# Holding back the first weight load, and moving tile 3's transposes into the fifth weight tile, in a fused LayerNorm + S5 + Mish MLP kernel

## The chip, the cores and the metric

One core of one Trainium2 chip. The metric is the device time of one execution in microseconds (us). Before the change it was 621.98 us, the median of three runs (621.54 to 622.13).

## The reference

```python
x  = A_x                                   # (1, 2048, 1024) bf16
xn = layernorm(x)                          # per token, over 1024
# A: diagonal complex state-space layer, 1024 states, plus a skip
Lam_bar = exp(dt * Lam);  B_bar = ((Lam_bar - 1) / Lam)[:, None] * Bmat
h_t = Lam_bar * h_{t-1} + B_bar @ xn_t
A   = 2 * Re(C h) + xn * Dskip
# B: dense, Mish, dense; w1 is 1024 x 3584, w2 is 3584 x 1024
z   = xn @ w1 + b1
B   = (z * tanh(softplus(z))) @ w2
out = x + A + B
```

## The kernel before

Tokens are worked in four blocks of 512, each block as four x tiles of 128 tokens. In each block TensorE does `xn @ w1` (28 weight tiles of 8 matmuls), the state-space input projection (128 matmuls), and then the second dense layer together with the output projection (352 matmuls). Weights come from HBM through a ring of seven slots; the first four weight tiles need slots 0 (contraction rows 0 to 511) and 1 (rows 512 to 1023), the next four slots 2 and 3.

TensorE does the matrix products and the transposes, VectorE and ScalarE the statistics, the scaling and the copies, and SyncE issues the loads. Only block 0's start-up matters here. Loads are issued in this order:

```python
    for h in range(2):                       # x tile 0, in two halves of the columns
        SP.dma(... xx[:, 0, 0, h * 512:(h + 1) * 512] ...)
    load_x(SP, 0, 1)                         # x tile 1
    ...
    for i in range(NRING):
        ring_load()                          # weight load i, 512 KB
        if i == 0:
            load_x(SP, 0, 2)                 # x tiles 2 and 3 behind weight load 0
            load_x(SP, 0, 3)
        ...
```

TensorE begins with filler matmuls on an identity matrix, so that they and not the real work take the slow stretch at the start: in the profile before, a 128-column filler took 107 ns up to 5.93 us and 56 ns from there. VectorE takes the statistics of tiles 0 and 1, scales them, and TensorE transposes them. Tiles 2 and 3 arrive later, so the first weight tiles are cut in two token halves: the first 256 tokens need only x tiles 0 and 1.

```python
    keep_busy(48)                            # filler: 128-column matmuls
    PE.op(... transpose of the small parameters ...)
    keep_busy(12)
    ...                                      # statistics, scale, transposes, copies of tiles 0 and 1
    first_mean_a(3)                          # ScalarE: sum of tile 3
    ...
    NSPLIT = 5
    def first_half(f, half, k0=0, k1=NK):    # 256 tokens of weight tile f: one matmul per k
        ...
    for f in range(4):
        first_half(f, 0, 0, NK // 2)         # 16 matmuls, weight load 0
    for f in range(4):
        first_half(f, 0, NK // 2, NK)        # 16 matmuls, weight load 1
        if f in (1, 3):
            q = 2 + f // 2
            first_transpose(q)               # tiles 2 and 3
            first_copy(q, VE)
    for f in range(4, NSPLIT):
        first_half(f, 0)
    ...                                      # then first_half(f, 1) for f < NSPLIT, whole tiles after
```

## Time and profile before

| | before |
|---|---|
| time, median of 3 | 621.98 us |
| profiled execution: time, span | 622.33 us, 620.9 us |
| share of TensorE in the chain of waits | 98% |
| x tile 1 landed (trace) | 5.50 us |
| first weight matmul | 9.46 us |

The first view is the chain of waits of the kernel before: start, length, what ended last there. Read it downwards. Everything up to 9.46 us is one dependence: x tile 1's load, its statistics, its scaling, the copy of its transpose. From there the chain is TensorE's own work nearly to the end, with one gap of 0.04 us at 13.66.

```profile
...
1.72 3.79 DMA xx<-in_A_x_dram
...
5.53 0.70 DVE stats L348
...
7.91 0.73 DVE xn L376 x2
8.64 0.67 DVE xnT L401 x2
...
9.46 2.78 PE ps L516 x24
...
14.32 5.33 PE ps L516 x48
19.64 39.71 PE ps L661 x184
59.36 27.63 PE ps L682 x128
...
```

The second view is the timeline of TensorE's matmuls (start, time, line, shapes, count). L388 are transposes, L516 the half-token matmuls, L661 the whole weight tiles.

```profile
...
9.46 2.78 PE L516 MATMUL ps<-xnT,ring 128*128 128x256 bf16 x24
12.17 0.62 PE L388 MATMUL ps<-ident,xn 128*128 128x128 bf16 x8
12.62 1.04 PE L516 MATMUL ps<-xnT,ring 128*128 128x256 bf16 x8
13.70 0.62 PE L388 MATMUL ps<-ident,xn 128*128 128x128 bf16 x8
14.16 5.49 PE L516 MATMUL ps<-xnT,ring 128*128 128x256 bf16 x48
19.48 2.75 PE L661 MATMUL ps<-xnT,ring 128*128 128x512 bf16 x12
```

The third is the timeline of the weight loads into TensorE's array (PEld), which adds in brackets how long that unit sat idle and what ended it.

```profile
...
12.16 0.45 PEld L388 LDWEIGHTS ps<-ident,xn 128*128 128x128 bf16 x8 [0.21 <-DVE xn L376]
...
13.69 0.45 PEld L388 LDWEIGHTS ps<-ident,xn 128*128 128x128 bf16 x8 [0.32 <-DVE xn L376]
...
15.10 4.26 PEld L516 LDWEIGHTS ps<-xnT,ring 128*128 128x128 bf16 x40 [0.19 <-DVE xnT L401]
...
```

### The profile page before, as it was taken

Reading aid. Unit: us, or ns where it says so; the run is one execution under the profiler, and the core shown is the slowest. Engines: PE = TensorE matmul, PEld = TensorE weight load, DVE = VectorE, ACT = ScalarE, POOL = GpSimd, SP = SyncE. Lnnn points to the kernel's source line nnn. Section 1 sums busy time; section 2 is a strip of 40 time slices with the busy share of each in tenths; the row PEclk is TensorE's granted clock in tenths of the full one; section 3 lists DMA queues with packets and bytes.
Section 4 is the critical chain, followed back from the end, with each engine's and each line's share of the span. In section 5 each row is a group of like instructions: output and inputs, shape, how many; then the busy total and the mean of one; then the engine's idle time right before and its main releaser. Section 6 shows DMA issues by size and latency. Waiting matters only on the chain.

```text
span 620.9 us, 7382 instructions
## 1 busy us (share of the span) xinstructions
PE 616.8 (99%) x2961; PEld 287.4 (46%) x2961; DVE 462.3 (74%) x676; ACT 247.9 (40%) x161; POOL 50.7 (8%) x47
## 2 busy tenths in 40 slices
PE   8999999999999999999999999999999999999998
PEld 7544444444444444444444444444444444444444
DVE  6897899999457599998147759999624856999603
ACT  5689996440069940000008992000000999000000
POOL 1999000000100000000010000000000000000000
DMA  9999966850365400784054430276203552033001
GB/s 293 258 269 258 220 110 187 207 150 0 117 193 165 136 0 25 209 191 119 17 187 135 141 131 1 75 209 170 90 35 103 163 176 68 1 123 115 1 0 69
DMA packets 95805, 79.41 MB, mean 128 GB/s; under 512 B 48923, under 2 KB 78235, under 8 KB 95771
## 3 DMA queue, kind: packets, MB, share of 16 engines
q1 hardware_dynamic: 92272, 71.64, 42.4%
q10 hardware_dynamic: 2538, 4.14, 1.8%
q0 software_dynamic: 960, 3.15, 1.6%
q8 instruction: 24, 0.39, 0.3%
q14 instruction: 11, 0.08, 0.0%
HBM read 63.19 MB, written 4.19 MB: 109 GB/s over the span
## 4 chain that ended last, share of the span: by engine, by line
PE 98%; DVE 1%; DMA 1%; SPq 0%; issue 0%
PE ps L740 49%; PE ps L661 30%; PE ps L682 18%; PE ps L516 1%; DMA xx<-in_A_x_dram 1%; DVE stats L348 0%; PE ps L754 0%; DVE xn L376 0%; PE ps L388 0%; SPq L291 0%; DVE xnT L401 0%; DVE xx L808 0%; DVE mv L353 0%; DVE par L495 0%; DVE rs L372 0%
## 5 line engine op out<-in xcount | busy, mean ns | idle before, releaser
L740 PE MATMUL ps<-ring,act 128*128 128x512 bf16 x896 | 194.0, 379 | 0.0
L661 PE MATMUL ps<-xnT,ring 128*128 128x512 bf16 x856 | 185.4, 379 | 0.0
L640 ACT ACTIVATE act<-hb 128x3584 bf16<-128x3584 bf16 x16 | 51.0, 3185 | 224.2 <-DVE hb L669 223.8
L740 PEld LDWEIGHTS ps<-ring,act 128*128 128x128 bf16 x896 | 87.7, 98 | 105.7
L661 PEld LDWEIGHTS ps<-xnT,ring 128*128 128x128 bf16 x856 | 83.7, 98 | 100.8
L669 DVE TENSOR_SCALAR hb<-ps,par 128x512 bf16<-128x512 f32 x112 | 82.5, 747 | 55.9 <-PE ps L661 54.7
L682 PE MATMUL ps<-xnT,BT 128*128 128x512 bf16 x512 | 111.2, 379 | 0.0
L740 PE MATMUL ps<-CT,hT 128*128 128x512 bf16 x506 | 109.9, 379 | 0.0
L687 DVE TENSOR_TENSOR mt<-ps,tab 128x1024 bf16<-128x1024 f32 x64 | 75.4, 1220 | 17.2 <-PE ps L682 16.6
L682 PEld LDWEIGHTS ps<-xnT,BT 128*128 128x128 bf16 x512 | 50.1, 98 | 60.4
L740 PEld LDWEIGHTS ps<-CT,hT 128*128 128x128 bf16 x506 | 49.5, 98 | 59.7
L705 DVE TENSOR_TENSOR_SCAN hT<-cs,qi,hT 128x512 bf16<-128x512 f32 x48 | 58.9, 1269 | 0.0
L785 DVE TENSOR_TENSOR xx<-ps,xx 128x1024 bf16<-128x1024 f32 (+1 forms) x16 | 18.8, 1190 | 46.3 <-PE ps L740 46.2
L642 ACT ACTIVATE act<-act 128x3584 bf16<-128x3584 bf16 x16 | 51.1, 3192 | 0.2
L641 ACT ACTIVATE act<-act 128x3584 bf16<-128x3584 bf16 x16 | 51.1, 3192 | 0.2
L710 DVE TENSOR_TENSOR mt<-hT,tab 128x1024 bf16<-128x1024 bf16 x64 | 41.4, 688 | 1.1
L647 DVE TENSOR_TENSOR act<-act,hb 128x3584 bf16<-128x3584 bf16 x16 | 32.3, 2018 | 1.3 <-ACT act L642 1.3
L287 POOL DMA_DIRECT2D xx<-in_A_x_dram x12 | 6.7, 560 | 253.2 <-DVE xx L785 146.2
L616 ACT ACTIVATE ct<-CT,cs 128x512 f32<-128x512 bf16 x16 | 11.5, 721 | 26.6 <-DVE CT L618 25.9
L641 ACT ACT_TABLE_LOAD x16 | 20.5, 1283 | 0.3
L642 ACT ACT_TABLE_LOAD x16 | 20.5, 1283 | 0.3
L705 DVE TENSOR_TENSOR_SCAN hT<-cs,hT 128x512 bf16<-128x512 f32 x16 | 18.7, 1209 | 0.0
(85 smaller groups left out, 276.8 us busy)
## 6 DMA issues: line engine op xcount, KB each, us to landing
ring<-in_B_w_dram SPq DMA_DIRECT2D x112, 512.0 KB, 4.1
out_dram<-xx ACTq DMA_DIRECT2D x15, 256.0 KB, 2.1
xx<-in_A_x_dram POOLq DMA_DIRECT2D x12, 256.0 KB, 3.6
xx<-in_A_x_dram SPq DMA_DIRECT2D x3, 256.0 KB, 4.9
xx<-in_A_x_dram SPq DMA_DIRECT2D x2, 128.0 KB, 2.2
dsk<-in_A_Dskip_dram SPq DMA_DIRECT2D x1, 256.0 KB, 8.4
xnT<-xn SPq DMA_TRANSPOSE x12, 4.7
BT<-in_A_B_re_dram SPq DMA_TRANSPOSE x8, 5.9
```

The costliest lines, as they stand in the source:

```text
L640: aop(lambda e: e.activation(a, hs, AF.Exp), reads=[b_hb[g % 2]], writes=[b_act[g]])
L641: aop(lambda e: e.activation(a, a, AF.Ln, bias=1.0), reads=[b_act[g]], writes=[b_act[g]])
L642: aop(lambda e: e.activation(a, a, AF.Tanh), reads=[b_act[g]], writes=[b_act[g]])
L647: vop(lambda e: e.tensor_tensor(a, a, hs, op=ALU.mult), reads=[b_act[g], b_hb[g % 2]], writes=[b_act[g]])
L661: PE.mm(lambda e, k=k, w=w: e.matmul(ps[:, bank, :], lhsT=w, rhs=xnT[:, k, :], start=k == 0, stop=k == NK - 1), reads=[b_ring[s]] + b_xnT, ...
L669: vop(lambda e: e.tensor_scalar(hb[:, hs, :], ps[:, bank, :], b1(f), None, op0=ALU.add), reads=[b_ps[bank], b_par], writes=[b_hbf[hs]])
L682: PE.mm(lambda e, j=j, ci=ci, k=k, bank=bank: e.matmul(ps[:, bank + ci, :], lhsT=BT[:, ci, j, k, :], rhs=xnT[:, k, :], start=k == 0, stop= ...
L687: vop(lambda e, s=s, u=u, j=j: e.tensor_tensor(mt[:, s, :, :], u, tab[:, s, j, :].unsqueeze(1).to_broadcast([P, 2, TB]), op=ALU.mult), rea ...
L705: vop(lambda e, ci=ci, init=init: e.tensor_tensor_scan(out=hT[:, ci, j, :], data0=cj("r", j).to_broadcast([P, TB]), data1=hT[:, ci, j, :], ...
L710: vop(lambda e, s=s: e.tensor_tensor(mt[:, s, :, :], hT[:, :, j, :], tab[:, s, j, :].unsqueeze(1).to_broadcast([P, 2, TB]), op=ALU.mult), ...
L740: PE.mm(lambda e: e.matmul(ps[:, u, :], lhsT=lhsT, rhs=rhs, start=st_, stop=last), reads=reads, writes=[b_ps[u]], first=st_, last=last)
L785: vop(lambda e: e.tensor_tensor(xr, src, xr, op=ALU.add), reads=b_ps[bank:bank + n] + [b_x], writes=[b_x])
```

## The change

It has two parts. **The hold:** SyncE waits until the first half of x tile 0 has landed before it issues the first weight load, the aim being that x tile 1 has the DMA engines to itself. **The reorder:** tile 3's transposes move from behind the fourth weight tile to the middle of the fifth, so that TensorE has more to do before it asks for them, and six instead of five weight tiles are cut in token halves, so that more stands between the transposes and the first use of their copy.

```diff
-    for h in range(2):
+    x0_events = [
         SP.dma(... x tile 0, half h ...)
+        for h in range(2)]
     load_x(SP, 0, 1)
+    SP.wait(x0_events[:1])
 ...
-    NSPLIT = 5
+    NSPLIT = 6
 ...
     for f in range(4):
         first_half(f, 0, NK // 2, NK)
-        if f in (1, 3):
-            q = 2 + f // 2
-            first_transpose(q)
-            first_copy(q, VE)
-    for f in range(4, NSPLIT):
-        first_half(f, 0)
+        if f == 1:
+            first_transpose(2)
+            first_copy(2, VE)
+    first_half(4, 0, 0, NK // 2)
+    first_transpose(3)
+    first_copy(3, VE)
+    first_half(4, 0, NK // 2, NK)
+    first_half(5, 0)
```

More of the change, by code (lines that the diff above doesn't have):

```diff
@@ L288, in load_x @@
                   s_xx[i][q] if blk else s_x0[q], writes=[b_xx[i][q]])
-    for h in range(2):
+    x0_events = [
         SP.dma(lambda e, h=h: e.dma_start(xx[:, 0, 0, h * 512:(h + 1) * 512], A_x[0, 0:P, h * 512:(h + 1) * 512]),
-               DmaSem(nc, "d_x00_%d" % h), writes=[b_xx[0][0].parts[h]])
+               DmaSem(nc, "d_x00_%d" % h), writes=[b_xx[0][0].parts[h]]) for h in range(2)]
     load_x(SP, 0, 1)
+    SP.wait(x0_events[:1])
     for src, r0, n in ((A_log_dt, 2 * NJ, NJ), (A_Lambda_im, NJ, NJ), (A_Lambda_re, 0, NJ),
```

## The prediction

> **What bounds the kernel now.** TensorE. The chain of waits shows it for 98% of the 620.9 us span; from 9.46 us on it is TensorE alone, at 48.35/224 = 216 ns per 512-column matmul in every block. What the start-up gains or loses passes to the end one for one. The change touches only the first 20 us.
>
> Start-up (chain, timeline): x tile 0's statistics end at 4.61. VectorE idles 0.68 us until x tile 1 lands at 5.50 (issued 1.72, so 3.8 us; tile 0's halves took 2.2). Then statistics, scale, transposes, copies, first weight tile at 9.46. TensorE then stops three times: 0.21 us (12.16, scaled tile 2), 0.32 (13.69, scaled tile 3), 0.19 (15.10, copy of transposed tile 3): 0.72 us. Half-width matmuls step at 4.28/40 = 107 ns, so 16 cost what 8 full ones do: the sixth half-token tile is free in itself.
>
> **A, the hold.** SyncE issues the first weight load at about 3.12 instead of 2.19; all loads behind it are issued 0.9 us later. Packet times show tile 1 mostly moved by 4.3; one engine was stuck 1.16 us on one packet and ended at 5.1. [...] the hold helps only if the stall comes from the weight load's start: 65%, I think. Then tile 1 lands at 4.2 to 4.6, the 0.68 us idle shrinks to 0.05, and the first weight tile starts at about 8.8.
> Cost: DMA idles near 4 to 5 us. The first four weight loads (6.94, 10.17, 11.66, 13.18 now) and x tiles 2 and 3 (7.59, 8.66) land 0.4 to 0.9 us later. The second load is needed 16 half-width matmuls (1.7 us) after the start, at 10.5 if A works, but lands near 10.8: a new stop of 0.2 to 0.4 us. Tile 3's statistics on ScalarE start up to 0.3 us late.
>
> **B, the reorder.** 24 matmuls, transposes of tile 2, 8 matmuls, 4 of the fifth weight tile, transposes of tile 3, 4 more of the fifth, 8 of the sixth, then the second token half. Tile 3's transposes are asked for 4 x 107 = 0.43 us later, covering the 0.32 us stop; 12 matmuls (1.28 us) follow before the second half, where the copy takes 0.69, covering the 0.19. Gain 0.51 us. Risk: the fourth load (13.18 plus the shift) is needed near 13.8.
>
> **Sum.** A: -0.65 at 65%, +0.2 to +0.35 for late weights. B: -0.5. Centre -0.7.
>
> **Predicted: 621.3 us, range 620.6 to 621.95.** Faster by over 2%: 0.005; within 2%: 0.99; slower: 0.005.
>
> **What the profile would show.** A right: the second statistics pair starts at 4.7 to 4.9 without a wait, first weight matmul at 8.7 to 8.9. A wrong: it still starts near 5.5. Late weights: a stop near 10.5, between the first halves' two row groups. B right: no stops before tile 3's transposes and before the second token half; 96 half-width matmuls instead of 80; full-width tiles begin at about 19.6 (19.48 + 0.86 for the added halves, minus the gain). Later blocks unchanged: 75.97, 48.35 and 27.63 us.
>
> **What would make it wrong.** A landing time that varies between runs by as much as the gain; the hold shifting the weights by the full 0.9 us, so that stops eat the gain; tile 1's landing not depending on the weights.

-0.65 at 65%, +0.2 to +0.35, and -0.5 come to the centre of -0.7, rounded; the 65% was the author's estimate.

## The result, and the profile after

The changed kernel took 621.60 us, the median of six runs (621.42 to 621.92), against 621.82 for six runs of the kernel before (621.54 to 622.13). The ratio of the fast runs is 0.9997 with a 95% interval of 0.9984 to 1.001: the same. A ratio is the mean time of one kernel's fast runs over that of the other's in the same rounds, so it is not quite the ratio of the medians. All these runs were fast (a run counts as slow when it lies over 1.5% above the fastest of its kernel), at a granted clock of 1.00.

The profiled execution took 621.73 us, span 620.3. Its chain of waits answers to the first fence above (line numbers moved by one to three):

```profile
...
1.42 5.29 PE ps L473 x48
6.71 0.13 PE ps L478
6.84 0.78 PE ps L473 x12
7.62 0.24 PE ps L389 x4
...
7.88 0.43 DVE xnT L402
...
8.90 1.91 PE ps L517 x16
10.81 0.04 issue
10.85 1.05 PE ps L517 x8
...
14.20 6.55 PE ps L517 x60
20.75 37.99 PE ps L664 x176
58.74 27.63 PE ps L685 x128
...
```

Two things differ from before. The start-up no longer hangs on x tile 1: its load is not in the chain. In its place stands TensorE's own filler, 48 matmuls that took 5.29 us and ended at 6.71. And the first 24 half-token matmuls are cut 16 and 8, with a stop between. The timeline of the matmuls after, and then two lines of that of the array's weight loads:

```profile
...
8.90 3.00 PE L517 MATMUL ps<-xnT,ring 128*128 128x256 bf16 x24
11.83 0.62 PE L389 MATMUL ps<-ident,xn 128*128 128x128 bf16 x8
12.28 1.47 PE L517 MATMUL ps<-xnT,ring 128*128 128x256 bf16 x12
13.59 0.61 PE L389 MATMUL ps<-ident,xn 128*128 128x128 bf16 x8
14.04 6.71 PE L517 MATMUL ps<-xnT,ring 128*128 128x256 bf16 x60
20.59 1.67 PE L664 MATMUL ps<-xnT,ring 128*128 128x512 bf16 x7
```

```profile
...
10.85 0.77 PEld L517 LDWEIGHTS ps<-xnT,ring 128*128 128x128 bf16 x8 [0.32 <-DMA ring<-in_B_w_dram]
11.82 0.45 PEld L389 LDWEIGHTS ps<-ident,xn 128*128 128x128 bf16 x8 [0.20 <-DVE xn L377]
...
```

The second weight load had landed at 10.81 us (10.17 before), and TensorE waited for it. In this pair of profiles x tile 1 landed at 4.41 instead of 5.50 us and the span fell by 0.6 us. On that evidence alone the hold looks like a success that paid for itself. The experiments say otherwise.

### The profile page after: what moved, and what is told of

The parts are those of the page before. It is cut to its first block, busy times and chain, and to the rows that moved or that the text cites. A ratio compares the mean times of both kernels' runs of the same rounds, so it can differ in the third digit from the quotient of the medians.

```text
span 620.3 us, 7398 instructions
## 1 busy us (share of the span) xinstructions
PE 616.7 (99%) x2969; PEld 288.5 (47%) x2969; DVE 462.2 (75%) x676; ACT 247.7 (40%) x161; POOL 50.4 (8%) x47
## 3 DMA queue, kind: packets, MB, share of 16 engines
q0 software_dynamic: 960, 3.15, 1.8%
## 4 chain that ended last, share of the span: by engine, by line
PE 99%; DVE 0%; POOL 0%; issue 0%; POOLq 0%
PE ps L743 49%; PE ps L664 30%; PE ps L685 18%; PE ps L517 2%; PE ps L473 1%; PE ps L757 0%; PE ps L389 0%; DVE xnT L402 0%; DVE xx L811 0%; POOL ident L333 0%; POOL ident L332 0%; PE ps L478 0%; DVE par L496 0%; POOL kon L336 0%; POOLq L885 0%
```

## The experiments

### How they are read

Twelve experiments ran, on eight different kernels. All gave correct results, and all timed runs counted as fast; a single look at one core has an unknown state by rule, but its granted clock was 1.00 too. Times vary by several tenths within a kernel, so I read four moments from each trace: **landing** of x tile 1 (its sixteenth completion), the time TensorE got **warm** (a name only, for the time from which its 128-column filler matmuls step at 56 ns and no longer at 107; the first step behind the parameter transpose is 66 or 67 ns when warm), the **first** weight matmul, and the **marker**, the start of the first matmul of block 0's input projection. (The expectations of the first eight runs quote the marker from the chain of waits, whose pieces start 0.16 us later: 59.36 and 58.74 there are 59.20 and 58.58 here. Differences are of the rounded moments and can be 0.01 off.)

| kernel, trace | tile 1 landed | 2nd weight load landed | warm | first | marker | marker - first | time - marker |
|---|---|---|---|---|---|---|---|
| before | **5.50** | 10.17 | 5.93 | 9.46 | 59.20 | 49.74 | 563.13 |
| before, second (e5) | 4.62 | 9.59 | 4.76 | 8.57 | 58.31 | 49.74 | 563.16 |
| before, third (e12) | 4.66 | 9.69 | **7.48** | 9.20 | 58.95 | 49.75 | 563.16 |
| hold only (e2) | 4.57 | 10.63 | **7.38** | 9.15 | 58.89 | 49.74 | 563.14 |
| hold only, second (e11) | 4.50 | 10.62 | 4.48 | 8.56 | 58.55 | 49.99 | 563.16 |
| reorder only (e1) | 4.53 | 9.79 | 4.25 | 8.54 | 57.99 | 49.45 | 563.14 |
| reorder only, second (e9) | 4.57 | 9.68 | **6.80** | 8.93 | 58.38 | 49.45 | 563.15 |
| reorder, 40 fillers (e7) | 4.43 | 9.83 | 6.55 | 8.54 | 57.99 | 49.45 | 563.14 |
| reorder, transposes later (e8) | **5.17** | 10.24 | 5.01 | 9.12 | 58.56 | 49.44 | 563.17 |
| reorder, x loads first (e4) | **4.86** | 9.60 | 5.20 | 8.81 | 58.27 | 49.46 | 563.14 |
| both (after) | 4.41 | 10.81 | **6.78** | 8.90 | 58.58 | 49.68 | 563.15 |
| both, second (e3) | 4.54 | 10.86 | 5.94 | 8.56 | 58.53 | 49.97 | 563.16 |
| both, third (e10) | 4.55 | 10.66 | **6.98** | 8.98 | 58.44 | 49.46 | 563.16 |
| both, longer hold (e6) | 4.39 | 12.73 | **7.20** | 9.09 | 60.40 | 51.31 | 563.17 |

The last column is the same to 0.04 us for every kernel: from the marker on nothing ever differs, and all variation of the time is made before it. The column before it shows what each part of the change does, free of the luck of the start.

### Theories

Theory 1, that of the prediction: the start of the first weight load delays x tile 1, and the hold takes that away. Theory 2: tile 1's landing at 5.50 us in the first profile was an unlucky draw; the hold does nothing for the usual landing and costs by making the weights late.

### e1: the reorder alone

```diff
     load_x(SP, 0, 1)
-    SP.wait(x0_events[:1])
```

> The reorder without the hold. Marker for all runs: the start of block 0's input projection in the chain of waits, 59.36 us before and 58.74 after; from there to the end every kernel should be the same. Theory 1 (the start of the first weight load disturbs x tile 1, so the hold is what brings it early): tile 1 lands at 5.2 to 5.7, first weight matmul 9.3 to 9.6, no stop before the transposes of tile 3 nor before the second token half, marker 58.8 to 58.9, time 0.4 to 0.6 us under before. Theory 2 (tile 1's landing at 5.50 was chance, the hold does nothing for it): tile 1 lands near 4.4 here too, first weight matmul near 8.9, second weight load at 10.2 so no stop there, marker 58.4 or less.

Measured: 621.35 us median (621.07 to 622.27, 5 runs), before 621.70 on the same chip, ratio 0.9994 (0.9982 to 1.0007). Tile 1 landed at 4.53 us with no hold at all. Its chain:

```profile
...
4.75 0.57 DVE stats L348
...
8.54 2.78 PE ps L516 x24
11.32 0.54 PE ps L388 x8
11.86 1.31 PE ps L516 x12
13.17 0.45 PE ps L388 x8
13.62 6.55 PE ps L516 x60
20.17 37.99 PE ps L663 x176
58.16 27.63 PE ps L684 x128
...
```

No stop on weights (the second load landed at 9.79), the whole stretch from the first matmul 0.29 us shorter than before (49.45 against 49.74). As theory 2 has it; theory 1's landing of 5.2 to 5.7 did not come.

### e2: the hold alone

The kernel before, with only the diff's first part.

> The hold without the reorder. Theory 1: tile 1 lands at 4.3 to 4.6, first weight matmul 8.8 to 9.0, a stop of about 0.3 us on the second weight load near 10.6, then the stops of 0.3 and 0.2 us before the transposes of tile 3 and the second token half as in before; marker near 59.0, time 0.3 us under before. Theory 2: the same here; this run only shows whether the early landing repeats with the hold.

Measured: 621.80 us (621.56 to 622.49, 5 runs), before 621.70, ratio 1.0001 (0.9988 to 1.0014). Tile 1 at 4.57, no better than in e1 without the hold. The second weight load came late (10.63), but TensorE was later still: warm only at 7.38, first weight matmul at 9.15, needing the load at 10.9. So the expected stop did not show, and the expected start at 8.8 to 9.0 was missed, both for a reason I had not thought of: the filler.

### e3: both parts again

The changed kernel, unaltered.

> The changed kernel unaltered, on the same chip as its two halves. Tile 1 at 4.3 to 4.6, first weight matmul 8.8 to 9.0, stop of 0.2 to 0.4 us on the second weight load, marker 58.6 to 58.9, time 0.2 to 0.6 us under before. If the landing varies by chance (theory 2), tile 1 may land anywhere from 4.2 to 5.6.

Measured: 621.69 us (621.40 to 623.48, 5 runs), before 621.70, ratio 1.0004 (0.999 to 1.0018). Here TensorE was warm early and began at 8.56, below the range I gave. It gained nothing by it:

```profile
...
8.56 1.91 PE L517 MATMUL ps<-xnT,ring 128*128 128x256 bf16 x16
10.90 1.05 PE L517 MATMUL ps<-xnT,ring 128*128 128x256 bf16 x8 [0.43 <-DMA ring<-in_B_w_dram]
```

The seventeenth matmul, the first that needs the second weight load, started 2.34 us after the first; without a stop it is 1.74 (e1: 8.54 to 10.28). That is 0.60 us of waiting for weights, of which 0.08 was made up at the transposes of tile 2: marker minus first is 49.97, 0.52 above e1.

### e4: x tiles first, no hold

```diff
-    SP.wait(x0_events[:1])
 ...
+    load_x(SP, 0, 2)
+    load_x(SP, 0, 3)
     for i in range(NRING):
         ring_load()
-        if i == 0:
-            load_x(SP, 0, 2)
-            load_x(SP, 0, 3)
```

> The reorder, no hold, but x tiles 2 and 3 are issued ahead of the first weight load, so the queue is never idle and the second weight load keeps its place. Theory 1 (it is the weight load's start that disturbs tile 1): tile 1 lands at 4.3 to 4.7 because a plain x load follows it; tiles 2 and 3 land near 6 and 7, first weight load near 8.7, second near 10.2; first weight matmul 8.8 to 9.0, no stop at 10.6, marker 58.3 to 58.5, time 0.7 to 1.0 us under before. Rival (any load that starts behind tile 1 disturbs it): tile 1 lands at 5.2 or later, first weight matmul near 9.4, marker near 58.8.

Measured: 621.41 us (621.08 to 622.23, 5 runs), before 621.70, ratio 0.9995 (0.9983 to 1.0008). Tile 1 landed at 4.86, between the two theories' values, the second weight load at 9.60, and there was no stop. The first weight load was issued at 3.15 us here, later than with the hold (3.00), and yet the second weight load came 1.2 us earlier than in the changed kernel. So late issue of the weights is not what costs; an idle queue is. The traffic between 4 and 5 us shows it. Two rows each of the view by stretches of time, of the changed kernel and then of e1: after the stretch come the busy time and count of PE, PEld, DVE, ACT and POOL, then the granted clock, the DMA share and GB/s:

```profile
...
4.00:5.00 1.00, 1.00 (x12) 1.00 (x10) 0.96 (x3) 0.22 (x1) 0.00 (x0) 1.00 0.54 111
5.00:6.00 1.00, 1.00 (x13) 1.00 (x11) 0.97 (x2) 0.08 (x1) 0.00 (x0) 1.00 0.89 284
...
```

```profile
...
4.00:5.00 1.00, 1.00 (x19) 1.00 (x18) 0.96 (x3) 0.22 (x1) 0.00 (x0) 1.00 0.97 304
5.00:6.00 1.00, 1.00 (x19) 0.86 (x17) 0.97 (x2) 0.08 (x1) 0.00 (x0) 1.00 1.04 363
...
```

By 10 us 2.27 MB had moved with both parts and 2.64 MB in e1: 0.37 MB, a microsecond at the 372 and 377 GB/s that they reach between 9 and 10 us. (The column before the DMA share is TensorE's granted clock. It reads 1.00 although the changed kernel's fillers step at 107 ns here; it does not show the warm-up, because the view counts time for which the trace has no clock record as full; the first record in this trace begins at 6.69 us, beside the 6.78 read from the steps.)

### e5: the kernel before, looked at again

> The kernel before, unaltered, looked at once more, because its only profile so far has tile 1 landing at 5.50 us while the reorder without the hold had it at 4.53 with the very same loads. Theory 1 (the first weight load delays tile 1): 5.2 to 5.7 again, first weight matmul 9.3 to 9.6, marker 59.2 to 59.4. Theory 2 (that landing was an unlucky one of a varying quantity, and the hold does nothing for it): 4.3 to 4.9, first weight matmul 8.5 to 9.0, marker 58.6 to 58.9, span 620.0 to 620.4 us.

Measured: 621.47 us, tile 1 at 4.62, first weight matmul at 8.57, span 620.0. The kernel before, unchanged, did what I had predicted of the hold. Theory 1 falls as an account of the usual run. The packet records of the first profile show what was unusual there: one packet of tile 1, of 2,048 bytes, took 1.16 us where the others of that load mostly took 0.08. Fifteen of the load's sixteen completions had come by 4.68 us, the last at 5.50.

### e6: a longer hold

```diff
-    SP.wait(x0_events[:1])
+    SP.wait([b_xx[0][1].parts[0].writer])        # x tile 1 whole
```

> The changed kernel with a longer hold: SyncE waits for the whole of x tile 1 instead of the first half of tile 0. Theory 2 (the hold only costs, through late weights): first weight load issued near 4.5 instead of 3.0, tile 1 still at 4.3 to 4.7, first weight load lands near 9, second near 12.2; the first weight matmul waits for weights until about 9.1, the stop before the second load grows to 1.2 to 1.8 us, marker 59.8 to 60.3, span 621.3 to 621.9. Theory 1 would have tile 1 land earlier still, at 4.0 to 4.2, but expects the late weights too; so the run mainly measures what a microsecond of hold costs.

Measured: 623.57 us, span 622.1, worse than I had expected. The first weight load was issued at 4.41 instead of 3.00 us, the second landed at 12.73. Tile 1 was at 4.39, no earlier than with the short hold.

```profile
...
9.09 1.91 PE L517 MATMUL ps<-xnT,ring 128*128 128x256 bf16 x16
12.78 1.05 PE L517 MATMUL ps<-xnT,ring 128*128 128x256 bf16 x8 [1.78 <-DMA ring<-in_B_w_dram]
...
```

1.41 us more of hold made the second weight load 1.92 us later, and marker minus first 51.31, 1.86 above e1. The suspected cost, made larger, stands in the place where theory 2 puts it.

### e7: the reorder with a shorter filler

```diff
-    keep_busy(48)
+    keep_busy(40)
```
(and no hold)

> The reorder without the hold, and 40 instead of 48 filler matmuls at the start. If the filler (4.16 to 5.30 us in five traces, ended by TensorE warming up at a time that varies) is at times what the first transposes wait for, its end comes 0.45 us earlier (8 warm steps of 56 ns) and the first weight matmul then hangs on tile 1 alone: 8.4 to 8.6 when tile 1 lands at 4.5; marker 58.1 to 58.3, median time 0 to 0.3 us below the reorder alone. If the filler never matters without the hold: same as the reorder alone, 621.1 to 621.5. [...]

Measured: 621.15 us (621.10 to 621.52, 5 runs), before 621.58 on this chip, ratio 0.9995 (0.9983 to 1.0008). TensorE got warm only at 6.55 in this trace, and still began at 8.54, as early as any. In e9 with 48 fillers it got warm at 6.80 and began at 8.93. Three rows of e7's timeline of matmuls, the filler, the transposes of tiles 0 and 1 and the first weight matmuls:

```profile
...
1.41 4.45 PE L472 MATMUL ps<-ident 128*128 128x128 bf16 x40 [1.41 <-POOL kon L335]
...
6.94 1.24 PE L388 MATMUL ps<-ident,xn 128*128 128x128 bf16 x16
...
8.54 2.78 PE L516 MATMUL ps<-xnT,ring 128*128 128x256 bf16 x24
...
```

The filler does not stand in e7's chain of waits. That chain begins with the load of x tile 0, issued at 0.79, and runs from there through VectorE's work on tiles 0 and 1, with no wait for tile 1. That of e5, an early start with 48 fillers, does the same. In the chain of e9 the filler's 5.30 us stand at the head, as in the changed kernel's. The 16 transposes and 24 matmuls after e7's warm-up took 1.24 and 2.78 us, as in e1. This is the lowest median, though the interval does not separate it from the others.

### e8: both groups of transposes four half-width matmuls later

```diff
-        if f == 1:
+        if f == 2:
             first_transpose(2)
             first_copy(2, VE)
-    first_half(4, 0, 0, NK // 2)
+    first_half(4, 0)
     first_transpose(3)
     first_copy(3, VE)
-    first_half(4, 0, NK // 2, NK)
     first_half(5, 0)
```
(and no hold)

> The reorder without the hold, with the transposes of tile 2 behind the third instead of the second weight tile's half, and those of tile 3 behind the whole fifth. Removing the hold left one stop, about 0.5 us before the transposes of tile 2; 4 more half-width matmuls (0.43 us) ahead of them should cover most of it, and 8 (0.86 us) remain to cover tile 3's copy (0.69 us plus waits). Expected: that stop 0.0 to 0.15 us, perhaps a new one of up to 0.1 us before the second token half; marker 57.7 to 57.9 when tile 1 lands near 4.5; median time 0.3 to 0.5 us below the reorder alone, so 0.7 to 0.9 us below before. Rival (time does not follow the marker): no change in the marker's distance to the end but the median stays at 621.3.

Measured: 621.76 us (621.56 to 622.02, 5 runs), before 621.58, ratio 1.0004 (0.999 to 1.0017). A miss. Marker minus first is 49.44, as in e1, e4, e7 and e9: the 0.5 us stop that I meant to cover was not there. I had added up bracketed idle times that belong to tile 0's transposes, which stand before the first weight matmul. In this trace tile 1 also landed late (5.17, without the hold), so the kernel began at 9.12.

### e9 and e10: reorder alone and both, once more on one chip

Kernels as e1 and as the changed kernel.

> The reorder without the hold a second time, beside the whole change on one chip, because the landing of tile 1 varies. In the ten traces so far time minus marker was 563.13 to 563.17 us, so each timed run tells its own start-up. Theory 2 (the hold does nothing for tile 1 in the usual run and costs by late weights): tile 1 at 4.4 to 4.7 in most runs, second weight load at 9.6 to 9.9 without a stop, median 621.0 to 621.4, 0.3 to 0.5 us below the whole change of this call. A middle theory (the hold takes away rare bad landings): more spread here than in the whole change, with some runs 0.5 us or more above the median.

> The whole change again. Theory 2: tile 1 at 4.4 to 4.6, second weight load at 10.6 to 10.9, a stop of 0.3 to 0.7 us in front of it, median 621.5 to 621.8. Middle theory: tile 1 never above 4.7 and a narrow spread of times. A theory in which the hold helps would have this median below that of the reorder alone.

Measured: 621.60 us for the reorder alone (621.34 to 621.94, 5 runs) and 621.63 for both (621.26 to 621.84, 5 runs), before 621.73; both ratios 0.9999. The expected 0.3 to 0.5 us between them did not appear. In both traces TensorE was warm late (6.80, 6.98) and began at 8.93 and 8.98. It then needed the second weight load at about 10.7, when even the held one (10.66) is there: marker minus first is 49.45 and 49.46. So the hold costs nothing in an execution whose start is late anyway, and theory 2 as I had put it was too simple.

### e11 and e12: one more look each at hold only and at before

> One look at the hold alone, for where tile 1 lands: with the hold so far 4.41, 4.57, 4.54 and 4.39; without it 5.50, 4.53, 4.62, 4.43, 5.17. Middle theory: again 4.3 to 4.7. If it lands above 4.9, the hold does not even take away bad landings. Time minus marker 563.1 to 563.2.

> One more look at the kernel before. Theory 2: 4.4 to 4.7 as in the second look, with a chance of some one in three of a landing above 4.9. Time minus marker 563.1 to 563.2.

Measured: hold only 621.71 us, tile 1 at 4.50; before 622.11 us, tile 1 at 4.66. In e11 TensorE was warm at 4.48 and began at 8.56; the held weights stopped it and marker minus first is 49.99, 0.25 above before's. In e12 tile 1 was on time, and the kernel was slow all the same, because TensorE was warm only at 7.48:

```profile
...
1.42 5.30 PE ps L472 x48
6.71 0.16 PE ps L477
6.87 1.05 PE ps L472 x12
...
9.20 2.78 PE ps L516 x24
...
```

## Why the prediction was right or wrong

The time fell inside the range, in its upper third (621.60; the centre was 621.3). That says little for the mechanism, since the range, 620.6 to 621.95, also held the time of the kernel before (621.82): it was wide enough for the hold to do nothing, and as far as the hold goes, meeting it was luck. The predicted gain of 0.7 us was too large; the measured medians differ by 0.2, less than the noise. The account that the runs support is a sum of three terms. Estimated from the table: time = 563.15 + first + 49.74, minus 0.29 with the reorder, plus 0 to 0.5 with the hold.

**The hold's benefit: wrong.** The step "tile 1 lands at 4.2 to 4.6, the 0.68 us idle shrinks to 0.05, and the first weight tile starts at about 8.8", credited with -0.65 at 65%, took one profile's landing for the kernel's. Landings without the hold, with the loads in before's order, were 5.50, 4.62, 4.66, 4.53, 4.57, 4.43 and 5.17 (median 4.62); with it, counting e6, 4.41, 4.54, 4.55, 4.57, 4.50 and 4.39 (median 4.52). VectorE could not have used more: it is busy with tile 0 until then and starts tile 1's statistics at 4.67 in the changed kernel's profile and in e1's alike. Nor did a weight load queued behind it hold tile 1 up as a rule: without the hold it landed at 4.43 to 4.66 in five of these seven traces.

What the late landings share is a slow packet. In all three of them (5.50, 5.17, and 4.86 in e4, where x tile 2 and not a weight load was next) a 2,048-byte packet of x, started after 2.6 us and before tile 1 had landed, took 0.99 us or more; in the other eleven traces the longest such packet took 0.56. All three were without the hold. Whether the hold takes such packets away (three of eight traces without, none of six with) is open; so few traces can't say, nor why a packet takes so long.

**What replaced tile 1 at the head of the chain: not foreseen.** The first weight matmul stood at 8.54 to 8.57 when TensorE was warm by 5.94 and tile 1 had landed by 4.66, or with 40 fillers (e7); at 8.90 to 9.20 in the six traces with 48 fillers where it was warm at 6.78 or later; at 8.81 to 9.46 in the three where tile 1 landed at 4.86 or later. Cold, a filler matmul takes 107 ns, warm 56; a late warm-up lets 48 of them end at 6.7 (e12) instead of 5.6 us (e1), and the parameter transpose, 12 more fillers and then the real transposes queue behind them. The step goes from 107 to 56 ns at times from 4.25 to 7.48 us over the fourteen traces, 3.2 us apart, with the filler always starting at 1.41 or 1.42: 2.8 us after the first filler in e1, 6.1 in e12. So the start of the filler does not fix the time of the change. What fixes it, and whether the filler has a part in it, was not shown. e7 supports the account of the queue from the other side, in one trace: fewer fillers and a late warm-up, yet an early start.

**Late weights: right, at the upper end.** Predicted 0.4 to 0.9 us later with a stop of 0.2 to 0.4 near 10.5. Medians of the second weight load are 10.66 us with the short hold (five traces) and 9.79 without (seven, loads in before's order): 0.9 later, so hardly any of the idle was absorbed. The stop was 0.2 us in the first profile, 0.6 in e3, 0.4 in e11 and none in e2 and e10. It grows as TensorE starts earlier, so the held weights set a floor of 10.7 to 10.9 us under the seventeenth matmul.

**The reorder: right in kind, mis-sized.** Predicted 0.51 us, measured 0.29 (49.74 to 49.45, equal within 0.02 in every trace of either kind without a weight stop). The term came from adding the idle times of the array's weight-load unit. Part of such an idle is the ordinary pace of loads behind matmuls, during which TensorE streams. In the matmul timeline before, 8 half-width matmuls (0.86 us) take 1.08 from 12.62 to the transposes at 13.70, a stop of 0.22 and not 0.32; in e1 12 of them (1.28) take 1.31, from 11.70 to 13.01, so 0.19 is won there. The stop before the second token half was read as 0.19, but little of it went: from 14.16 to 19.48 is 5.32 us for 48 matmuls (48 x 0.107 = 5.14) before, from 13.46 to 20.01 is 6.55 for 60 (6.42) in e1, 0.05 less over. The rest is 0.02 us for 16 half-width matmuls (1.71) in place of 8 full ones (1.73), and rounding.

**Small points.** Later blocks are unchanged as predicted (time minus marker), and there are 24 + 12 + 60 = 96 half-width matmuls. "Full-width tiles begin at about 19.6" was an arithmetic slip: a sixth split tile adds both its halves, 16 x 107 ns = 1.71 us, so 19.48 + 1.71 - 0.6 gives the 20.59 that was seen.

**The whole.** With an early start (8.54) the sum gives, as estimates, 621.43 for before, 621.14 for the reorder and 621.66 for both; with a late warm-up (8.98) 621.87, 621.58 and 621.59. The two parts help and harm in different executions, and the medians of a few runs mix them. The traces favour the reorder without the hold and with 40 fillers (e7: 621.15 against 621.58 on its chip), but by a gain that the timed runs alone do not establish. The hold with 40 fillers, which by this account should meet the late weights more often, was not run.

## What to carry to other kernels

Before building on a wait of a few tenths of a microsecond, profile the same kernel two or three times: the one landing that this change was aimed at did not repeat. Compare distances between two fixed instructions in the trace, not total times, when a start-up effect is smaller than the spread of runs. Read TensorE's stops from the starts of its matmul groups against their count times their step, not from the idle of the weight-load unit (here 0.32 us of idle beside a stop of 0.22); and remember what the held-back queue cost here: 111 instead of 304 GB/s between 4 and 5 us, and a second weight load 0.9 us later.
